# A new order of the steps in a kernel of sliding-window attention and a two-layer MLP

## The chip, the cores and the metric

The kernel runs on one core of one Trainium2 chip. A core has a matrix engine (TensorE, PE in the profile), three engines for elementwise work (VectorE = DVE, ScalarE = ACT, GpSimd = POOL) and SyncE (SP), which here only issues DMAs. Each engine takes its own instructions strictly in order; semaphores let one engine wait for another or for a transfer. TensorE writes its results into PSUM, eight banks of 512 f32 columns on 128 partitions; everything else on the core lies in SBUF. The metric is the device time of one execution in microseconds (us).

## The reference

```python
B, H, S, D = 8, 8, 576, 64          # q, k, v: f32
scores = (1 / sqrt(D)) * q @ k.T     # per batch and head
mask = (rel >= 0) & (rel < 64)       # rel = query position - key position
attn = softmax(where(mask, scores, -1e9))
x = (attn @ v).transpose(0, 2, 1, 3).reshape(B * S, H * D)     # 4608 x 512
h = x @ w_in                         # w_in 512 x 2048
g = h - tanh(h)
out = g @ w_out                      # w_out 2048 x 512, out f32
```

A query sees itself and the 63 keys before it. The token rows that attention gives are the input of the MLP.

## The kernel before

**Tiling.** Heads go in pairs: batch b has four pairs, g = 4b to 4b + 3, 32 in all. A pair's 576 queries are nine windows of 64, and a window needs the 128 keys up to its end. The 4608 tokens of the MLP are nine chunks c of 512, and the 2048 hidden columns are 16 tiles m of 128. All products are in bf16, with f32 in PSUM. Batch b fills tokens 576b to 576b + 575, so chunk c needs the batches up to the one that holds its last token: chunk 4, for example, spans batches 3 and 4.

**Stages of a batch.** Loads go through GpSimd's DMA queue and turn f32 into bf16 on the way for batches 3 to 7. Batches 0 to 2 turn keys and queries round with TensorE (steps Fp, Ep) and copy them out of PSUM (Fc, Ec); the rows that lk, lq load for a pair are rearranged by ck, cq first (function cast, L126; called casts below). Batches 3 to 7 load token rows (lr for keys, qr for queries, L166, the second number being one of five blocks of 128 tokens) and turn them round by DMA transposes on SyncE's queue (tk, L171, into kw; tq, L179, into qw). LV (L145) loads a block of values, and Z, za, zb (L151, L152, function move) copy the rows that windows need on the other half of the partitions. tz copies the tail of q.

**Steps on TensorE.** S.g (L299, L304) makes the scores of pairs g and g + 1 of batches 3 to 7; Rp (L286) those of one pair and half of its windows in batches 0 to 2. PP.g (L348) multiplies the probabilities of two pairs by the values. Xp (L397) turns attention rows round for batches 0 to 2; from batch 3 on Y.b.half (L416, two DMA transposes each) does so on SyncE's queue. H.c.m (L431) is the first layer of chunk c and tile m: four matmuls of 512 columns, with PSUM bank m mod 2 for c > 1. Hp.c.m.half (L508) is one half of such a step, which needs only one half of the chunk's columns (Y.b.0 or Y.b.1). W.c.s.part (L474) is a quarter of the second layer for 128 tokens: four matmuls of 512 columns into bank 2; the quarters of one s can come in any order. The last s of the last chunk is cut by columns (L467).

**Steps on the other engines.** ScalarE: A.c.m (tanh, L439), Sx.g.part (the exp of parts 0, 1 and, of the ninth window, 2; L314), Rx (L318). VectorE: G.c.m (h - tanh(h), L445, which frees H's bank), M.g (masking the probabilities in place, L323), DR.g and DN.g.n (reciprocal, three normalisations, L365, L368). O.c.s.engine copies a finished second-layer tile out of PSUM on ScalarE (L90) or VectorE (L92), and SyncE stores it (L495; three buffers). Xc, Fc, Ec, ck, cq, za, zb and tz name their engine as their last letter: a ScalarE, v VectorE, p GpSimd.

**What sets the order.** Nothing is scheduled by a program: one long string, PLAN (from L537, played by play, L532), lists the steps. Each word is a step, looked up in STEPS (L518), and its instructions go to the end of their engine's queue, DMAs to that of SyncE or GpSimd. The string thus fixes the order on every engine; the waits between engines follow from the buffers that the steps share.

```python
    def play(script):
        for word in script.split():
            what, *args = word.split(".")
            STEPS[what](*[ENG[a] if a in ENG else int(a) for a in args])
```

The lines that matter below: the end of chunk 0's first layer (L554), the casts ck.9 to cq.11 (L557 to L562), tz.3 (L571), batch 5's transposes tk.5, tq.5 with Y.4 (L579 to L585), and Sx.22, which begins behind A.4.4 (L590).

Of the kernel before, what the change touches and what calls it, by code (L numbers as in the profile page):

```python
# [15 lines left out]
def kernel(  # L16
# [515 lines left out]
    def play(script):  # L532
# [30 lines left out]
        A.1.3 Rx.10.1.3 H.1.4 A.1.4 G.1.3 Ec.11.6.a H.1.5 A.1.5 qr.3.0 Z.2 H.1.6 qr.3.2 PP.8 G.1.5 Rp.11.0.3
        A.1.6 tk.3.1 tq.3.3 lr.3.0 H.1.8 Rx.11.0.3 G.1.4 G.1.6 DR.8 H.1.7 DN.8.2 A.1.8 A.1.7 H.1.9 tq.3.1 G.1.8
        H.1.11 G.1.7 A.1.9 tk.3.4 H.1.10 lr.3.3 A.1.11 A.1.10 DN.8.1 G.1.9 Rp.11.1.3 Rx.11.1.3 Rp.10.0.6 tq.3.2
        G.1.11 DN.8.0 G.1.10 Rx.10.0.6 H.1.12 tq.3.0 M.10 H.1.14 A.1.12 M.11 H.1.13 Xp.2.0.1.3 Xp.2.0.0.4 G.1.12
        A.1.13 A.1.14 Xc.2.0.1.3.a PP.10 H.1.15 LV.4.1 LV.3.1 A.1.15 Xc.2.0.0.4.a LV.3.3 G.1.13 LV.3.2 LV.3.0
# [5 lines left out]
        M.13 tk.4.3 tq.4.4 G.2.5 A.2.4 PP.12 W.1.2.3 H.2.7 lr.6.4 lr.5.4 DR.12 DN.12.2 G.2.4 tq.4.3 tk.4.2
        tq.4.1 lr.6.3 DN.12.0 A.2.7 lr.5.3 lr.5.1 lr.5.0 tq.4.2 DN.12.1 H.2.6 G.2.7 qr.5.2 S.14 H.2.9 A.2.6
        Sx.14.2 Sx.14.1 A.2.9 tk.5.4 Sx.14.0 G.2.6 G.2.9 M.14 M.15 qr.6.0 W.1.2.0 H.2.8 W.1.2.1 W.1.2.2
        Xp.3.0.1.3 A.2.8 G.2.8 tq.5.3 H.2.11 O.1.2.v PP.14 DR.14 H.2.10 A.2.11 A.2.10 Xc.3.0.1.3.v G.2.10
        Xp.3.0.0.4 W.1.3.2 G.2.11 tq.5.4 W.1.3.3 H.2.12 A.2.12 H.2.13 Z.4 A.2.13 W.1.3.1 G.2.12 G.2.13 H.2.14
# [73 lines left out]
```

## Time and profile before

| | |
|---|---|
| median of 3 runs | 307.63 us (307.45 to 307.67) |
| the profiled execution: span from the first to the last instruction | 305.2 us |
| TensorE busy | 297.8 us, 98% |
| VectorE busy | 176.2 us, 58% |
| ScalarE busy | 157.5 us, 52% |
| GpSimd busy | 103.7 us, 34% |
| granted TensorE clock | 1.000 |
| moved by DMA | 36.77 MB, mean 120 GB/s |

The profile is of one execution; all durations below are from it, and its span is the time from its first to its last instruction. PE is TensorE's matmuls, PEld its weight loads, which run beside the matmul in front. An entry such as "L474 PE MATMUL ps<-w_out_sb,gT" names the line of the kernel, the engine, the operation, and output <- inputs by the program's names. In a list of groups, "xN | busy, mean ns | idle before, releaser" gives a group's count, its busy time, the mean of one, and the idle time of the engine in front of it with what ended most of it. In a timeline the first number is the start in us from the span's start, the second what the row's instructions took together, and [..] an idle time before them. A matmul's end is modelled, so matmul records overlap. SPq and POOLq are the DMA queues' issuing instructions.

### The profile page before, as it was taken

To read this page: it belongs to the slowest core of one execution; us is meant where nothing else is said; L and a number is where in the kernel's file an instruction comes from. 1 tells how busy PE (TensorE), PEld (TensorE's weight loads), DVE (VectorE), ACT (ScalarE), POOL (GpSimd) and SP (SyncE) were. 2 spreads that over 40 slices of the span, in tenths; PEclk is the share of its full clock that TensorE was granted. 3 is DMA by queue.
4 is the path that set the end of the run, shared out by engine and by line. 5 is a ranking of instruction groups with operands and counts; after the bars stand their busy time and mean duration, and the time that the engine had idled before them with its cause. 6 is when DMAs were issued, how large, how long until landed. Compare 5 with 4: busy or idle time off the path is not lost.

```text
span 305.2 us, 6469 instructions
## 1 busy us (share of the span) xinstructions
PE 297.8 (98%) x2599; PEld 149.4 (49%) x2632; DVE 176.2 (58%) x316; ACT 157.5 (52%) x265; POOL 103.7 (34%) x141
## 2 busy tenths in 40 slices
...
DMA packets 132878, 36.77 MB, mean 120 GB/s; under 512 B 119920, under 2 KB 127344, under 8 KB 132848
## 3 DMA queue, kind: packets, MB, share of 16 engines
q0 software_dynamic: 92752, 18.06, 85.3%
...
HBM read 36.70 MB, written 9.44 MB: 151 GB/s over the span
## 4 chain that ended last, share of the span: by engine, by line
PE 87%; DVE 5%; ACT 3%; issue 2%; POOL 2%; DVEq 0%; ACTq 0%; POOLq 0%
PE ps L474 38%; PE ps L431 30%; PE ps L508 6%; PE ps L348 3%; PE ps L304 2%; DVE gT L445 2%; PE ps L397 1%; ACT th L439 1%; PE ps L286 1%; PE ps L467 1%; DVE pt L323 1%; PE ps L260 1%; PE ps L281 1%; PE ps L227 1%; POOL qall L110 1%
## 5 line engine op out<-in xcount | busy, mean ns | idle before, releaser
L445 DVE TENSOR_TENSOR gT<-ps,th 128x512 bf16<-128x512 f32 x144 | 97.2, 687 | 85.3 <-ACT th L439 84.6
L474 PE MATMUL ps<-w_out_sb,gT 128*128 128x512 bf16 x527 | 131.5, 380 | 2.2 <-issue 0.8
L439 ACT ACTIVATE th<-ps 128x512 f32<-128x512 f32 x144 | 84.7, 599 | 93.0 <-PE ps L431 79.7
L431 PE MATMUL ps<-xT,wi 128*128 128x512 bf16 x496 | 120.7, 380 | 0.1
L474 PEld LDWEIGHTS <-gT 128*128 128x128 bf16 x560 | 53.3, 98 | 61.4
L431 PEld LDWEIGHTS <-wi 128*128 128x128 bf16 x496 | 47.0, 98 | 54.3
L145 POOL DMA_DIRECT2D vw<-in_v_dram x35 | 30.0, 872 | 36.1 <-PE ps L348 33.5
L90 ACT ACTIVATE ysb<-ps 128x512 f32<-128x512 f32 (+1 forms) x24 | 14.2, 593 | 30.9 <-PE ps L474 30.2
L166 POOL DMA_DIRECT2D qall<-in_q_dram x25 | 21.7, 881 | 24.1 <-DMA qw<-qall 21.4
L166 POOL DMA_DIRECT2D kall<-in_k_dram x25 | 21.7, 875 | 10.4 <-DMA kw<-kall 4.8
L314 ACT ACTIVATE pt<-ps 128x1024 bf16<-128x1024 f32 (+1 forms) x30 | 23.3, 816 | 3.5 <-PE ps L304 3.2
L323 DVE TENSOR_TENSOR pt<-pt,ps 128x1152 bf16<-128x1152 bf16 x28 | 20.5, 749 | 5.1 <-ACT pt L314 3.2
L508 PE MATMUL ps<-xT,wi 128*128 128x512 bf16 x80 | 20.8, 380 | 0.0
L92 DVE COPY ysb<-ps 128x512 f32<-128x512 f32 (+1 forms) x11 | 7.1, 650 | 20.5 <-PE ps L467 13.2
L368 DVE TENSOR_TENSOR xs<-ps,rcp 128x384 bf16<-128x384 f32 x28 | 15.2, 550 | 0.3
L318 ACT ACTIVATE pt<-ps 128x640 bf16<-128x640 f32 (+1 forms) x24 | 14.7, 659 | 0.8 <-PE ps L286 0.8
L348 PEld LDWEIGHTS <-pt 128*64 128x64 bf16 x504 | 9.4, 112 | 6.3 <-DVE pt L323 2.1
L90 ACT ACTIVATE kt<-ps 128x576 bf16<-128x576 bf16 x10 | 6.5, 647 | 10.8 <-PE ps L256 6.8
L227 PE MATMUL ps<-warm 128*128 128x512 bf16 (+1 forms) x35 | 10.6, 435 | 1.1 <-DVE warm L207 1.1
L508 PEld LDWEIGHTS <-wi 128*128 128x128 bf16 x80 | 7.4, 98 | 8.5 <-issue 0.4
L348 PE MATMUL ps<-vw,pt 128*64 128x65 bf16 x504 | 11.0, 197 | 0.3 <-DVE pt L323 0.2
L365 DVE TENSOR_TENSOR xs<-ps,rcp 128x384 bf16<-128x384 f32 x14 | 7.7, 550 | 0.1
...
## 6 DMA issues: line engine op xcount, KB each, us to landing
...
vw<-in_v_dram POOLq DMA_DIRECT2D x28, 128.0 KB, 6.6
qall<-in_q_dram POOLq DMA_DIRECT2D x20, 128.0 KB, 7.5
kall<-in_k_dram POOLq DMA_DIRECT2D x20, 128.0 KB, 6.8
...
```

The source lines that it names most:

```text
L90: nc.scalar.activation(o, i, ACT.Copy)
L145: nc.gpsimd.dma_start(out=w[:, 2 * i + 1, :, 0:D] if i < NF else w[64:128, 2 * i, :, 0:D], in_=v[b, :, 128 * i:128 * i + n].rearrange("h p ...
L166: nc.gpsimd.dma_start(out=token_rows(b, n)[0:c, i], in_=(q if n == "q" else k)[b, :, 128 * i:128 * i + c].rearrange("h p d -> p h d"))
L314: nc.scalar.activation(o, sp, ACT.Exp, scale=scale)
L323: nc.vector.tensor_tensor(p, p, mask.unsqueeze(1).to_broadcast([128, 2 * NJ, 64]), ALU.mult)
L348: nc.tensor.matmul(ps[r, bank, 65 * i:65 * i + 65], PT[(g + r2) % NPT][:, j, r], vw[b % 2][:, j, p0 + r2 + NP * h, :], start=True, stop=True)
L368: nc.vector.tensor_tensor(xs[b % 2][:, p0 // 2, 0:6, n // 2, :], ov[:, :, 0:D], sums[g][:, n].to_broadcast([128, 6, D]), ALU.mult)
L431: nc.tensor.matmul(hp, w_in_tile(ki, m), chunk_tile(c)[:, n.start // 64:n.stop // 64, ki % 2, 64 * (ki // 2):64 * (ki // 2) + 64], start=( ...
L439: nc.scalar.activation(th[:, n], hp, ACT.Tanh)
L445: nc.vector.tensor_tensor(gT[c][:, m, columns(s)], hp, th, ALU.subtract)
L474: nc.tensor.matmul(yp, gT[c][:, m, s * 128:(s + 1) * 128], w_out_sb[:, m, :], start=n == 1 and i == 0, stop=n == 4 and i == 3)
L508: nc.tensor.matmul(hp, w_in_tile(half + 2 * i, m), chunk_tile(c)[:, :, half, 64 * i:64 * i + 64], start=n == 1 and i == 0, stop=n == 2 and ...
```

## The change

The first 230 words of PLAN stay. From "H.0.14 M.4" on (end of chunk 0's first layer, 37.6 us into the profiled span) all words come in a new order. They are the same steps with the same matmuls, transfers and buffers, but for three things: some steps go to another engine, some to another PSUM bank, and score steps of batch 2 are paired differently. Other engines: the casts ck.9, ck.10, ck.11 go from ScalarE to GpSimd and cq.10, cq.11 from VectorE to GpSimd; zb.1.3 from GpSimd to ScalarE, zb.1.2 from ScalarE to VectorE; tz.5 from VectorE and tz.6 from ScalarE to GpSimd, tz.7 from VectorE to ScalarE; and many of the copies O, Xc, Fc and Ec change between ScalarE and VectorE. The loads and transposes of batches 3 to 7 stand in longer runs of DMA steps between the others, and the quarters of the second layer stand in other places between first-layer steps.

```diff
-        Rx.7.1.3 cq.9.v H.0.14 M.4 wo.3 zb.1.3.p G.0.12 Ec.8.1.a PP.4 wo.1 A.0.14 H.0.15 mk DR.4 DN.4.1 G.0.14
-        A.0.15 H.0.13 DN.4.0 za.1.3.a W.0.0.0 Rp.8.0.3 G.0.15 A.0.13 Rp.8.1.5 DN.4.2 zb.1.2.a za.1.2.v Rx.8.1.5
-        W.0.1.0 M.7 qr.3.3 LV.2.3 lk.11.p PP.6 Rx.8.0.3 Xp.1.0.1.3 W.0.0.2 G.0.13 Xp.1.0.0.4 DR.6 Xc.1.0.1.3.a
-        DN.6.2 DN.6.0 W.0.1.2 DN.6.1 Xp.1.1.0.5 lk.10.p ck.9.a Xc.1.0.0.4.a Fp.9.3 Xc.1.1.0.5.a Xp.1.1.1.4
-        lr.3.2 lq.10.p lq.11.p LV.2.2 Hp.1.0.0 Ep.9.7 Xc.1.1.1.4.v Ec.9.7.a Fc.9.3.a Hp.1.0.1 W.0.1.3 W.0.0.3
-        qr.3.4 LV.2.0 Rp.9.1.5 Rp.9.0.3 LV.2.1 W.0.0.1 O.0.0.a M.8 LV.2.4 W.0.1.1 lr.3.1 lr.3.4 A.1.0 tq.3.4
-        G.1.0 O.0.1.a Rx.9.1.5 Rx.9.0.3 ck.11.a M.9 ck.10.a W.0.2.1 W.0.2.0 W.0.2.3 W.0.2.2 W.0.3.2 qr.3.1
...
-        Hp.1.2.1 Hp.1.2.0 Fc.10.7.a A.1.1 A.1.2 Rp.10.1.3 G.1.1 cq.11.v G.1.2 Fc.11.5.a H.1.3 Ep.11.6 tk.3.2
...
-        W.1.1.2 G.2.3 Hp.2.1.0 tz.3.a Hp.2.1.1 W.1.1.3 G.2.0 qr.4.2 qr.5.4 lr.5.2 H.2.2 A.2.1 G.2.1 S.12 A.2.2
...
-        G.2.14 W.2.0.2 Xc.3.1.1.7.v Xc.3.0.0.4.a Xc.3.1.0.6.a G.2.15 qr.5.0 Hp.3.0.0 W.2.0.3 Hp.3.1.1 Hp.3.1.0
-        O.2.0.a A.3.1 W.2.1.1 Hp.3.0.1 W.2.1.2 G.3.1 tz.4.v A.3.0 S.16 Sx.16.2 W.2.1.3 Sx.16.1 G.3.0 H.3.3
-        W.2.1.0 M.17 Sx.16.0 M.16 H.3.2 A.3.3 PP.16 G.3.3 O.2.1.a A.3.2 tk.5.2 qr.5.1 qr.6.4 H.3.5 LV.5.3
-        W.2.2.1 DR.16 A.3.5 tk.5.1 DN.16.2 tq.5.2 G.3.2 DN.16.1 H.3.4 DN.16.0 Y.4.0 A.3.4 S.18 G.3.5 W.2.2.0
-        H.3.7 G.3.4 Sx.18.1 A.3.7 Sx.18.2 G.3.7 W.2.2.3 H.3.6 A.3.6 Sx.18.0 tk.6.4 tk.5.3 tq.5.0 tq.5.1 H.3.9
-        tk.5.0 M.19 W.2.2.2 G.3.6 qr.7.1 H.3.8 M.18 A.3.9 PP.18 A.3.8 O.2.2.v G.3.9 DR.18 G.3.8 DN.18.2 DN.18.1
-        DN.18.0 W.2.3.0 W.2.3.3 H.3.11 qr.6.2 lr.6.0 LV.5.4 lr.6.2 LV.5.0 A.3.11 W.2.3.1 G.3.11 Y.4.1 tq.6.4
-        H.3.10 W.2.3.2 A.3.10 tq.6.2 G.3.10 O.2.3.a H.3.13 H.3.14 A.3.13 LV.5.1 LV.5.2 lr.6.1 qr.6.1 A.3.14
-        G.3.13 W.3.0.2 H.3.15 tz.5.v G.3.14 qr.6.3 H.3.12 W.3.0.0 A.3.15 G.3.15 Hp.4.1.0 A.3.12 G.3.12 Hp.4.1.1
-        A.4.1 W.3.0.1 G.4.1 W.3.0.3 Hp.4.0.1 H.4.3 Hp.4.0.0 O.3.0.v tk.6.3 tk.6.2 A.4.0 S.20 A.4.3 Sx.20.2
-        Sx.20.0 Sx.20.1 tq.6.0 tk.6.0 W.3.1.1 G.4.0 G.4.3 W.3.1.0 H.4.2 W.3.1.3 A.4.2 S.22 G.4.2 H.4.4 W.3.1.2
-        H.4.7 A.4.4 G.4.4 M.20 O.3.1.a Sx.22.0 Sx.22.1 A.4.7 W.3.2.1 H.4.6 W.3.2.2 A.4.6 Sx.22.2 W.3.2.3 Z.5
-        G.4.7 M.22 M.21 H.4.9 PP.20 G.4.6 tq.7.1 tq.6.1 A.4.9 tk.6.1 tq.6.3 W.3.2.0 O.3.2.a DR.20 DN.20.2 G.4.9
...
-        W.8.1.0 W.8.2.3 W.8.2.0 W.8.2.1 O.8.1.a W.8.3.2 O.8.2.a O.9.0.a W.8.3.0 W.8.3.1 O.8.3.v"""
+        Rx.7.1.3 cq.9.v H.0.14 M.4 Ec.8.1.a PP.4 wo.3 G.0.12 Rp.8.0.3 A.0.14 Rx.8.0.3 H.0.15 A.0.15 wo.1 lk.11.p
+        lq.10.p LV.2.2 qr.4.3 LV.2.4 qr.3.0 ck.9.p ck.11.p LV.2.1 LV.2.0 lk.10.p cq.10.p lq.11.p qr.4.4 LV.2.3
+        lr.3.4 lr.3.0 qr.3.4 ck.10.p cq.11.p lr.3.1 DR.4 G.0.14 DN.4.1 DN.4.2 DN.4.0 G.0.15 Ep.9.4 za.1.3.a
+        zb.1.3.a H.0.13 A.0.13 Ec.9.4.a za.1.2.v zb.1.2.v M.7 W.0.0.0 Xp.1.0.0.6 Xp.1.0.1.3 W.0.1.0 Xc.1.0.0.6.a
...
+        A.1.13 qr.3.1 LV.3.2 lr.4.0 qr.3.2 tq.4.3 LV.3.4 LV.3.0 qr.4.2 qr.3.3 lr.3.2 tq.3.1 tq.3.2 lr.3.3 LV.3.3
+        lr.4.4 LV.3.1 lr.4.1 tk.3.4 tq.3.4 LV.4.3 qr.4.1 qr.5.4 tk.3.1 tq.3.3 tq.3.0 tk.3.2 tk.3.3 tk.3.0 LV.4.2
+        qr.5.2 qr.4.0 lr.4.2 lr.5.0 tq.4.1 tq.4.4 lr.5.1 qr.5.3 LV.4.0 qr.5.1 lr.4.3 tk.4.0 tk.4.4 G.1.8 G.1.12
+        H.1.14 H.1.15 Xc.2.0.1.4.a G.1.13 Xp.2.0.0.3 W.1.0.1 W.1.0.2 A.1.14 A.1.15 tz.3.a Xc.2.0.0.3.a DR.10
+        G.1.14 DN.10.0 DN.10.2 Xp.2.1.0.7 Xc.2.1.0.7.a G.1.15 W.1.0.0 Hp.2.1.0 DN.10.1 Xp.2.1.1.7 Xc.2.1.1.7.a
...
+        M.17 G.3.7 M.16 Z.4 G.3.2 W.2.2.0 W.2.2.2 W.2.2.1 H.3.3 A.3.3 PP.16 H.3.8 DR.16 DN.16.0 G.3.3 W.2.2.3
+        A.3.8 H.3.9 G.3.8 DN.16.1 DN.16.2 O.2.2.a A.3.9 lr.5.4 lr.5.3 qr.6.2 LV.5.1 qr.6.0 lr.6.2 LV.5.4 LV.5.3
+        LV.5.2 qr.5.0 qr.6.3 lr.5.2 lr.6.1 qr.6.1 LV.5.0 lr.6.0 G.3.9 H.3.6 A.3.6 G.3.6 S.18 Sx.18.2 W.2.3.2
+        H.3.5 Sx.18.0 A.3.5 W.2.3.3 H.3.10 G.3.5 Sx.18.1 A.3.10 W.2.3.1 tq.5.2 tk.5.3 tk.5.2 tq.5.1 tq.5.0 Y.4.0
+        tk.5.4 lr.6.4 lr.6.3 M.18 Z.5 M.19 H.3.11 A.3.11 W.2.3.0 PP.18 G.3.11 DR.18 DN.18.1 G.3.10 DN.18.0
+        DN.18.2 Y.4.1 tk.6.4 tq.6.1 tk.6.1 LV.6.2 lr.7.2 qr.7.3 tq.6.0 tk.6.3 tk.6.2 tq.6.3 H.3.13 O.2.3.a
+        A.3.13 G.3.13 W.3.0.1 H.3.14 W.3.0.2 H.3.15 A.3.14 G.3.14 A.3.15 H.3.12 A.3.12 G.3.15 G.3.12 S.20
+        Sx.20.2 Sx.20.0 Sx.20.1 Hp.4.1.0 W.3.0.0 W.3.0.3 Hp.4.1.1 Hp.4.0.1 Hp.4.0.0 S.22 A.4.1 A.4.0 G.4.1 G.4.0
+        O.3.0.v H.4.9 A.4.9 H.4.2 A.4.2 G.4.2 G.4.9 M.21 M.20 W.3.1.3 W.3.1.0 W.3.1.2 H.4.3 H.4.4 W.3.1.1
+        Sx.22.2 Sx.22.1 A.4.3 A.4.4 G.4.3 G.4.4 H.4.7 H.4.6 A.4.7 A.4.6 O.3.1.v G.4.6 PP.20 DR.20 DN.20.2 G.4.7
+        W.3.2.0 H.4.10 A.4.10 DN.20.1 G.4.10 Sx.22.0 M.22 DN.20.0 M.23 W.3.2.2 H.4.5 A.4.5 G.4.5 W.3.2.1 H.4.8
+        W.3.2.3 A.4.8 lr.7.3 LV.6.1 qr.7.1 lr.7.1 qr.7.0 qr.7.4 qr.6.4 tq.7.4 tq.6.4 tq.7.3 LV.6.4 lr.7.0 PP.22
+        G.4.8 tk.6.0 lr.7.4 tk.7.4 tk.7.2 tq.6.2 LV.6.3 tk.7.3 O.3.2.v H.4.14 A.4.14 G.4.14 DR.22 H.4.11 A.4.11
...
+        W.8.1.1 W.8.1.0 W.8.2.0 W.8.2.3 W.8.1.3 O.8.2.a W.8.0.0 W.8.0.1 W.8.0.3 W.8.1.2 O.8.1.a W.8.3.2 W.8.0.2
+        W.8.3.3 O.8.0.v O.9.0.a W.8.3.1 W.8.3.0 O.8.3.a"""
```

More of the change, by code (lines that the diff above doesn't have):

```diff
@@ L563 @@
[L563 to L567, printed above, removed]
@@ L573 @@
[L573 to L577, printed above, removed]
```

77 lines of the change are left out of this document (43 added, 34 removed).

## The prediction

> **What bounds the kernel now.** I read the page first (span, busy shares, chain), then the timeline of the weight loads, because a matmul's record hides waits: records overlap, while a weight load starts once per matmul.
>
> ```profile
> span 305.2 us, 6469 instructions
> ...
> PE 297.8 (98%) x2599; PEld 149.4 (49%) x2632; DVE 176.2 (58%) x316; ACT 157.5 (52%) x265; POOL 103.7 (34%) x141
> ...
> PE 87%; DVE 5%; ACT 3%; issue 2%; POOL 2%; DVEq 0%; ACTq 0%; POOLq 0%
> ```
>
> TensorE sets the end. The next question is how much of its 298 us is waiting in disguise.
>
> ```profile
> 161.99 0.10 PEld L431 LDWEIGHTS <-wi 128*128 128x128 bf16 x1
> 162.51 0.66 PEld L348 LDWEIGHTS <-pt 128*64 128x64 bf16 x36 [0.42 <-issue]
> 163.20 0.55 PEld L474 LDWEIGHTS <-gT 128*128 128x128 bf16 x4
> 163.87 1.18 PEld L431 LDWEIGHTS <-wi 128*128 128x128 bf16 x6
> ...
> 285.06 5.06 PEld L474 LDWEIGHTS <-gT 128*128 128x128 bf16 x24
> 290.24 1.29 PEld L467 LDWEIGHTS <-gT 128*128 128x128 bf16 x8
> ```
>
> From 285.06 to 290.24 are 24 matmuls: 0.216 us each, so a step of four (H or W) is 0.863 us. A PV step (PP) starts 0.52 us after the last wide load instead of 0.216 (0.30 for the change of form), lasts 0.69, and the step behind it takes 0.67 instead of 0.863: net 0.80. Against these prices the waits stand out:
>
> ```profile
> 43.41 0.93 PEld L348 LDWEIGHTS <-pt 128*64 128x64 bf16 x36 [0.42 <-issue]
> ...
> 66.11 0.65 PEld L348 LDWEIGHTS <-pt 128*64 128x64 bf16 x36 [0.55 <-DVE vw L152]
> ...
> 90.14 0.36 PEld L348 LDWEIGHTS <-pt 128*64 128x64 bf16 x18 [0.47 <-DVE pt L323]
> 90.80 0.36 PEld L348 LDWEIGHTS <-pt 128*64 128x64 bf16 x18 [0.30 <-DVE pt L323]
> ```
>
> PP.6 takes 0.93 for 0.66 (0.27 lost), PP.8 begins 0.13 late, PP.12 loses 0.05 and 0.30. That is 0.75 us; I allow up to 1.1 for smaller gaps that I do not list. So from chunk 0's last steps on, the old order leaves TensorE waiting for about 0.8 us. **This is all that a new order can win**, since the same matmuls are issued.
>
> **The change part by part.** *TensorE's own work.* Counting runs of attention matmuls in both orders: 28 before, 27 after, because the score steps of batch 2 are paired differently and some stand right behind a PP. One change of form fewer is 0.3 at most; one old run stands behind transposes, a cheaper start, so I take -0.1 (bounds 0 and -0.3). The end (last quarter's columns, one small copy, one store) has the same steps in other clothes: 0.
>
> *The old waits.* I assume that all of them go: -0.8 (bounds 0 and -1.1).
>
> *A new wait at H.4.7.* In the new order ScalarE has "Sx.22.2 Sx.22.1 A.4.3 A.4.4" behind A.4.2. By the waits of the built kernel Sx.22.2 waits for M.20, in both orders; before, it stood behind A.4.7 and A.4.6, where this cost nothing. Now two tanhs are queued behind it, for them G.4.3, and for G.4.3 the bank of H.4.7.
>
> ```profile
> 147.05 1.29 DVE L445 TENSOR_TENSOR gT<-ps,th 128x512 bf16<-128x512 f32 x2 [1.66 <-ACT th L439]
> 156.90 1.42 DVE L323 TENSOR_TENSOR pt<-pt,ps 128x1152 bf16<-128x1152 bf16 x2
> ...
> 153.68 1.94 ACT L314 ACTIVATE pt<-ps 128x1024 bf16<-128x1024 f32 x2
> 155.49 1.11 ACT L439 ACTIVATE th<-ps 128x512 f32<-128x512 f32 x2
> 156.44 0.43 ACT L314 ACTIVATE pt<-ps 128x256 bf16<-128x256 f32 x1
> ...
> 280.10 1.89 PE L474 MATMUL ps<-w_out_sb,gT 128*128 128x512 bf16 x7
> 280.30 0.60 ACT L439 ACTIVATE th<-ps 128x512 f32<-128x512 f32 x1 [0.27 <-PE ps L431]
> 280.93 0.69 DVE L445 TENSOR_TENSOR gT<-ps,th 128x512 bf16<-128x512 f32 x1 [0.17 <-ACT th L439]
> ```
>
> The last three rows give the hand-over: a tanh starts 0.20 after the next step's matmuls have begun, lasts 0.60, the subtract follows after 0.03 and lasts 0.69. Back to back, subtracts and masks advance by 0.60 to 0.67 (two in 1.29, two in 1.42), a wide exp by 0.91. From the end of H.4.2 as zero: A.4.2 0.20 to 0.80; G.4.2 from 0.83, G.4.9 from 1.43, M.21 from 2.03, M.20 from 2.70 to 3.45; Sx.22.2 from 3.48, Sx.22.1 from 3.80, A.4.3 from 4.74 to 5.34; G.4.3 to 6.06. TensorE meanwhile has W.3.1.3, W.3.1.0, W.3.1.2, H.4.3, H.4.4 and W.3.1.1: 6 x 0.863 = 5.18. H.4.7 is late by **0.9**. (Were Sx.22.2 free earlier, this would be nothing.)
>
> *Batch 5's hand-over (S.20 and Hp.4.1.1).* SyncE's queue is in order. In the new order the transposes tq.5.2, tk.5.3, tk.5.2, tq.5.1, tq.5.0, two of Y.4.0 and tk.5.4 all stand behind the store O.2.2, that is behind W.2.2.3.
>
> ```profile
> 191.31 5.12 SPq L171 DMA_TRANSPOSE kw<-kall  x4
> 196.53 1.22 SPq L179 DMA_TRANSPOSE qw<-qall  x1
> ...
> 160.65 0.34 SPq L495 DMA_DIRECT2D out_dram<-ysb  x1
> 161.08 2.54 SPq L416 DMA_TRANSPOSE xT<-xs  x2
> ...
> 150.47 0.22 PE L299 MATMUL ps<-q,kw 128*128 128x64 bf16 x2
> 150.62 0.70 PE L304 MATMUL ps<-qw,kw 64*128 64x64 bf16 x34
> 151.25 1.04 PE L431 MATMUL ps<-xT,wi 128*128 128x512 bf16 x4
> ```
>
> A transpose takes 5.22 / 4 = 1.30 of the queue, a store 0.43, an S step 0.78. From the end of W.2.2.3: the copy O.2.2 ends at 0.80, its store is issued at 0.83, tk.5.4 at 1.26 + 7 x 1.30 = 10.4. S.20 wants it after 15 steps of 0.863, S.18 and PP.18: 14.5. It may take 4.1 to land. Y.4.1 follows PP.18's last norm (PP.18 ends at 9.55, and DR, three norms and G.3.10 take 2.4): issued at 12.0, wanted by Hp.4.1.1 at 14.5 + 0.78 + 0.43 + 2 x 0.863 = 17.5, so 5.5 to land. What do they take? Loads on GpSimd's queue decide:
>
> ```profile
> qw<-qall SPq DMA_TRANSPOSE x1, 2.4
> kw<-kall SPq DMA_TRANSPOSE x1, 2.4
> ...
> xT<-xs SPq DMA_TRANSPOSE x1, 4.9
> ...
> xT<-xs SPq DMA_TRANSPOSE x2, 6.0
> ...
> qw<-qall SPq DMA_TRANSPOSE x1, 6.6
> ...
> 135.91 1.76 POOL L166 DMA_DIRECT2D qall<-in_q_dram  x2 [21.40 <-DMA qw<-qall]
> ...
> 163.41 4.18 POOL L145 DMA_DIRECT2D vw<-in_v_dram  x5 [18.06 <-PE ps L348]
> ```
>
> These are windows of the DMA view: 133:135.4 (the first two), 136:137.3, 137.35:138.7, 138.8:140. A burst of loads starts at 135.91: in front of it transposes land in 2.4, just behind its start in 4.9, then in 6.0 to 6.6. In the new order the first load of a burst (LV.6.2) waits for PP.18, at 9.55: the start of a burst again follows a PV step, as at 163.41. So tk.5.4, 0.4 into the burst, takes about 4.9 (0.8 late) and Y.4.1, two into it, 6.0 to 6.6 (0.5 to 1.1 late, in place of the 0.8 and not on top). I take **0.9**; bounds 0 (all land in 2.4) and 2.5.
>
> *The same one batch later.* Y.5.0 and Y.5.1 are issued into the burst behind PP.22; by the same count they are 0 to 1.2 late for Hp.5.0.0; I take **0.4**.
>
> *Batch 2 and 3 loads.* Five casts go from ScalarE and VectorE to GpSimd, and ck.11, ck.10 and cq.11 there wait for loads to land, with all later loads queued behind them. At the far end ScalarE waits in tz.3.a for transpose tq.3.4, and Xc.2.0.0.3.a, which Hp.2.1.0 needs, is queued behind it.
>
> ```profile
> L92 POOL COPY vw<-vw 64x520 bf16<-64x520 bf16 x4 | 2.5, 620 | 2.3 <-DMA vw<-in_v_dram 2.2
> ...
> kall<-in_k_dram POOLq DMA_DIRECT2D x2, 128.0 KB, 8.7
> qall<-in_q_dram POOLq DMA_DIRECT2D x1, 128.0 KB, 8.1
> ```
>
> No cast on GpSimd is in this trace; from the copy, 0.62 for 520 elements, 768 elements are an estimated 0.9 each (bounds: 0.6, the copy itself, and twice 0.9). Loads beside transposes took 8.1 to 8.7 (window 58:60), else some 6 in the page's medians. With 0.9 and 7 I find the chain just in time at Hp.2.1.0; with 9 it is over 2 late. I take **0.3** (bounds 0 and 3). ScalarE and VectorE get room where the casts leave, but they are no bound there.
>
> [...]
>
> *Short bank waits in chunk 1* (H.1.12, where VectorE has subtracts, norms and a mask in a row): 0 to 0.4, taken 0.2.
>
> **Sum:** -0.8 - 0.1 + 0.9 + 0.9 + 0.4 + 0.3 + 0.2 = +1.8 us. The profiled span goes from 305.2 to 307.0; the median of the runs, 307.63, lies 2.4 above that span, and I keep this distance: **309.4 us**.
>
> **The rivals.**
> 1. *The transposes land in time*: bursts start a little later or the queue drains faster, as in the rows of 2.4. Then the old waits are only exchanged for H.4.7 and chunk 1: -0.9 + 0.9 + 0.2 = +0.2, 307.8 us. For it: 4.9 against 4.1 allowed is a near thing. Against: the burst is tied to PP.18.
> 2. *The other side, faster*: M.20 comes early enough that Sx.22.2 does not hold the tanhs, and transposes land in time too. The point is 0.9 us on M.20. Then only -0.9 remains, with a little left of chunk 1: 306.8 us at -0.8. Against: VectorE's five instructions from A.4.2 on have no gap to give.
> 3. *GpSimd's chain fails*: casts of 1.8 us, or blocked by VectorE, put 5 x 0.9 = 4.5 us on the load queue; some 2 of it are covered before Ep.11.7 and Hp.2.1.0. It decides from about 1 us. That is +2.5 on the forecast: 311.9 us. For it: three waits for landings in a row. Against: the four copies of 0.62 agree with each other although VectorE was busy beside them.
>
> [...]
>
> **How the numbers follow.** Forecast 0.45 (308.4 to 310.5), rival 1 0.27, rival 2 0.10, rival 3 0.18. A difference of 0.2% (0.6 us) is about what a measurement of this kernel can tell. Rival 2 is faster by more than that (0.10); rival 1 lies within it except for a tenth of it (0.24); the rest is slower (0.66). The range 307.0 to 311.9 leaves out rival 2 and the upper half of rival 3.
>
> **What would show it.** In the profile after: a gap in front of H.4.7's matmuls near 154 us with ScalarE's small exp waiting for L323; S.20 and Hp.4.1.1 waiting for DMA kw and xT near 141 to 146; ScalarE idle near 77 in front of the q copy. PP.6, PP.8 and PP.12 at 0.66 to 0.7 would show the old waits gone. I am wrong if transposes near a burst's start land in 2.4, if GpSimd's casts differ much from 0.9, or if a wait shows up at S.12 or S.16, where I count none.

## The result, and the profile after

The changed kernel takes 321.33 us (median of 4 runs, 320.19 to 322.74) against 307.65 us: 1.043 times the time before, 95% interval 1.040 to 1.047. That is 13.7 us slower, where 1.8 were forecast and 311.9 was the upper end of the range. The profiled execution took 322.74 us, the longest of the four, and its span is 15.7 us longer than that of before. Here and below, a kernel's time is the median of its fast runs, which leaves out single executions more than 1.5% above its fastest, and each ratio is taken against runs of the kernel before from the same session.

The page of the changed kernel, the rows that answer to those of before:

```profile
span 320.9 us, 6508 instructions
...
PE 306.4 (95%) x2632; PEld 151.5 (47%) x2632; DVE 177.5 (55%) x311; ACT 155.3 (48%) x264; POOL 109.3 (34%) x147
...
PEclk9999999999799999997899979999999999999999
...
PE 62%; DMA 21%; POOL 6%; SPq 4%; issue 3%; DVE 1%; ACT 1%; POOLq 0%; ACTq 0%
```

Two things are new. Transfers hold 21% of the chain that sets the end, where before it was 87% TensorE and no DMA. (This share alone proves little: p4_loads below, as fast as the kernel before, has 14%.) And the granted clock dips in three places. The same row of the kernel before:

```profile
PEclk9999999999999999999999999999999999999999
```

What TensorE waited for in the changed kernel (total, times, longest), then its weight loads around the four long waits:

```profile
PE ps L508 <- DMA xT<-xs: 3.4, 1, 3.4
PE ps L299 <- DMA kw<-kall: 3.0, 1, 3.0
PE ps L508 <- ACT xT L90: 2.0, 1, 2.0
```

```profile
81.97 0.10 PEld L508 LDWEIGHTS <-wi 128*128 128x128 bf16 x1 [2.33 <-issue]
...
84.09 0.15 PEld L508 LDWEIGHTS <-wi 128*128 128x128 bf16 x1 [0.28 <-issue]
...
148.92 0.13 PEld L299 LDWEIGHTS <-kw 128*128 128x128 bf16 x2 [3.49 <-DMA kw<-kall]
...
151.04 0.15 PEld L474 LDWEIGHTS <-gT 128*128 128x128 bf16 x1 [0.28 <-issue]
...
164.47 1.39 PEld L431 LDWEIGHTS <-wi 128*128 128x128 bf16 x7 [0.98 <-issue]
...
187.69 0.10 PEld L508 LDWEIGHTS <-wi 128*128 128x128 bf16 x1 [3.67 <-issue]
```

The numbers in brackets are the gaps in front of weight loads (PEld), which TensorE starts ahead of the matmuls (before S.20 the last weight load ended at 145.42, the last matmul at 145.92). In order they are those of Hp.2.1.0, S.20, H.4.7 and Hp.5.0.0. Of each gap 0.1 is there in any case (a load takes 0.10, and the next starts 0.216 after it), so they cost 2.2, 3.4, 0.9 and 3.6: 10.1 us. The rows at 84.09 and 151.04 show the rest: a weight load behind the wait starts 0.43 after the one before it (0.28 of gap and 0.15) instead of 0.216. TensorE works at half speed there. The windows view says from when to when; its last columns are the granted clock, the DMA share and GB/s:

```profile
83.00:83.50 0.50, 0.50 (x3) 0.20 (x2) 0.00 (x0) 0.50 (x2) 0.50 (x1) 0.59 1.71 158
86.25:86.50 0.25, 0.25 (x2) 0.13 (x1) 0.25 (x1) 0.00 (x0) 0.00 (x0) 0.50 2.27 148
86.50:86.75 0.25, 0.25 (x2) 0.10 (x1) 0.07 (x1) 0.00 (x0) 0.00 (x0) 0.99 1.84 206
147.50:148.00 0.50, 0.00 (x0) 0.00 (x0) 0.00 (x0) 0.00 (x0) 0.50 (x2) 0.95 2.21 165
154.40:154.80 0.40, 0.40 (x2) 0.15 (x1) 0.00 (x0) 0.00 (x0) 0.00 (x0) 0.53 3.63 131
188.50:189.00 0.50, 0.50 (x3) 0.20 (x2) 0.00 (x0) 0.00 (x0) 0.00 (x0) 0.91 2.17 165
192.25:192.50 0.25, 0.25 (x2) 0.10 (x1) 0.00 (x0) 0.25 (x1) 0.00 (x0) 0.86 0.88 176
```

A slice's mean gives the moment: 0.59 over 83.0 to 83.5 means that the clock fell from 1.00 to 0.50 at 83.09. It is at half from 83.09 to 86.50, 147.95 to 154.78 and 188.91 to 192.32: 3.41, 6.83 and 3.41 us, four stretches of one length. Less the 0.97 that TensorE still stood at S.20, it worked 12.7 us at half clock, which can cost 6.3 at most; 15.7 less the 10.1 of the waits leaves 5.6. The cost of the half clock can also be read directly, by timing the same steps of TensorE in an execution in which the clock stayed at 1.00: behind Hp.2.1.0 they took 4.55 us (2.86 in e1_tz3), from S.20 to S.22 6.55 (3.88 in p4_loads), behind Hp.5.0.0 4.93 (3.39 in p4_loads). That is 1.7, 2.7 and 1.5 us more, 5.9 in all. Waits and half clock thus make 16.0, beside the 15.7 measured. The small ones nearly cancel: of the old waits PP.12's is gone and PP.6's is not, and in chunk 1 the two Rp.10 steps cost 0.64 and the two of Rp.11 0.71, where two such steps cost 0.47 in the kernel before: 0.2 new each.

### The profile page after: what moved, and what is told of

Same layout as the page of the kernel before. It is cut to its first block, busy times and chain, and to the rows that moved or that the text cites. A ratio compares the mean times of both kernels' runs of the same rounds, so it can differ in the third digit from the quotient of the medians.

```text
span 320.9 us, 6508 instructions
## 1 busy us (share of the span) xinstructions
PE 306.4 (95%) x2632; PEld 151.5 (47%) x2632; DVE 177.5 (55%) x311; ACT 155.3 (48%) x264; POOL 109.3 (34%) x147
## 4 chain that ended last, share of the span: by engine, by line
PE 62%; DMA 21%; POOL 6%; SPq 4%; issue 3%; DVE 1%; ACT 1%; POOLq 0%; ACTq 0%
PE ps L474 29%; PE ps L431 22%; DMA wi<-in_moe_w_in_dram 5%; PE ps L508 4%; DMA qall<-in_q_dram 4%; DMA kall<-in_k_dram 3%; DMA xT<-xs 3%; DMA qw<-qall 2%; DMA vw<-in_v_dram 2%; PE ps L304 2%; SPq L179 2%; POOL vw L145 2%; DMA kw<-kall 2%; PE ps L348 2%; SPq L171 2%
## 5 line engine op out<-in xcount | busy, mean ns | idle before, releaser
L474 PE MATMUL ps<-w_out_sb,gT 128*128 128x512 bf16 x560 | 139.0, 386 | 0.0
L431 PE MATMUL ps<-xT,wi 128*128 128x512 bf16 x496 | 121.2, 379 | 1.0 <-DVE gT L445 0.9
L474 PEld LDWEIGHTS <-gT 128*128 128x128 bf16 x560 | 54.4, 99 | 64.4 <-issue 3.6
L145 POOL DMA_DIRECT2D vw<-in_v_dram x35 | 30.8, 889 | 16.1 <-PE ps L348 14.6
L508 PE MATMUL ps<-xT,wi 128*128 128x512 bf16 x80 | 23.0, 406 | 5.4 <-DMA xT<-xs 3.4
L92 DVE COPY ysb<-ps 128x512 f32<-128x512 f32 x17 | 11.7, 688 | 27.8 <-PE ps L474 27.8
L90 ACT ACTIVATE ysb<-ps 128x512 f32<-128x512 f32 (+2 forms) x18 | 10.3, 573 | 28.0 <-PE ps L474 24.6
L368 DVE TENSOR_TENSOR xs<-ps,rcp 128x384 bf16<-128x384 f32 x28 | 14.9, 550 | 0.2
L92 POOL COPY q<-qw 64x256 bf16<-64x256 bf16 x2 | 0.8, 398 | 33.7 <-DMA qw<-qall 33.7
L90 ACT ACTIVATE xT<-ps 128x512 bf16<-128x512 bf16 (+3 forms) x17 | 7.3, 486 | 4.4 <-PE ps L397 3.4
```

Of the source, the lines that this page charges most:

```text
L90: nc.scalar.activation(o, i, ACT.Copy)
L145: nc.gpsimd.dma_start(out=w[:, 2 * i + 1, :, 0:D] if i < NF else w[64:128, 2 * i, :, 0:D], in_=v[b, :, 128 * i:128 * i + n].rearrange("h p ...
L431: nc.tensor.matmul(hp, w_in_tile(ki, m), chunk_tile(c)[:, n.start // 64:n.stop // 64, ki % 2, 64 * (ki // 2):64 * (ki // 2) + 64], start=( ...
L474: nc.tensor.matmul(yp, gT[c][:, m, s * 128:(s + 1) * 128], w_out_sb[:, m, :], start=n == 1 and i == 0, stop=n == 4 and i == 3)
L508: nc.tensor.matmul(hp, w_in_tile(half + 2 * i, m), chunk_tile(c)[:, :, half, 64 * i:64 * i + 64], start=n == 1 and i == 0, stop=n == 2 and ...
```

## The experiments

My theory: the transfers stand where they land too late, and each long wait costs a half-clock stretch on top. Rivals: each late transfer is a separate accident; the clock falls for another reason; the new compute order itself asks for the impossible; the casts on GpSimd are to blame.

### One wait undone at a time

**e1_tz3.**

```diff
-... tz.3.a Xc.2.0.0.3.a ... Xc.2.1.1.7.a mk
+... Xc.2.0.0.3.a ... Xc.2.1.1.7.a tz.3.a mk
```

> The changed kernel with one word moved: tz.3.a (ScalarE, the copy that waits for transpose tq.3.4) goes from in front of Xc.2.0.0.3.a to behind Xc.2.1.1.7.a. In the changed kernel Hp.2.1.0 stood 2.2 us behind it, and from 83.1 to 86.5 us TensorE's granted clock was 0.50. Theory (each wait also costs the half-clock stretch that follows it, about 1.7 us): both go, 321.3 - 3.9 = 317.4 us, and the windows view shows a clock of 1.00 from 80 to 90. Rival A (the low clock comes for a reason of its own): only the wait goes, 319.1. Rival B (batch 3's transposes are late for every reader): S.12 waits instead, 321.

Measured: 318.87 us, ratio 1.039 (1.032 to 1.046), which overlaps the changed kernel's 1.040 to 1.047. Hp.2.1.0 no longer waits, and the clock is 1.00 from 60 to 90 us, as the theory said; but rival B comes true in part. The waits of e1_tz3:

```profile
PE ps L299 <- DMA kw<-kall: 3.5, 1, 3.5
PE ps L508 <- DMA xT<-xs: 2.1, 2, 1.7
PE ps L304 <- DMA kw<-kall: 1.6, 1, 1.6
```

The 1.6 at L304 is new: S.12, which had been spared because TensorE came to it later, now waits for tk.3.0. The 3.5 at L299 is S.20, and it speaks against the theory as I put it: TensorE's matmuls and the window around them show no half clock behind it.

```profile
142.38 1.89 PE L431 MATMUL ps<-xT,wi 128*128 128x512 bf16 x8
147.79 0.23 PE L299 MATMUL ps<-q,kw 128*128 128x64 bf16 x2 [3.52 <-DMA kw<-kall]
```

```profile
148.00:155.00 7.00, 6.89 (x96) 3.78 (x98) 1.98 (x3) 4.25 (x7) 2.75 (x4) 1.00 1.88 125
```

So not each long wait costs a half-clock stretch. The last section sets this one beside those that did.

**e2_tk54.**

```diff
-... W.2.3.1 tq.5.2 tk.5.3 tk.5.2 tq.5.1 tq.5.0 Y.4.0 tk.5.4 ...
+... W.2.3.1 tk.5.4 tq.5.2 tk.5.3 tk.5.2 tq.5.1 tq.5.0 Y.4.0 ...
```

> The changed kernel with tk.5.4 moved in front of tq.5.2, so that SyncE issues it first of its run of transposes, about 10 us earlier. Theory (two waits one behind the other): S.20 no longer waits 3.5 us, but the first half of Y.4.1, which landed at 151.2 in the changed kernel, is then late by about 2.8 for Hp.4.1.1, and a half-clock stretch follows it too: 321.3 - 1.5 = 319.8 us. Rival (tk.5.4 is the only late transfer here): 3.5 us of wait and some 2.5 of low clock go, 315.3.

Measured: 319.61 us, ratio 1.040 (1.031 to 1.049). The theory's 319.8 is met, but the interval holds that of the changed kernel: a gain is not shown. S.20 is cured, and the two halves of chunk 4's first step wait in its place, for Y.4.0 and Y.4.1. Weight loads of e2_tk54:

```profile
147.78 0.11 PEld L508 LDWEIGHTS <-wi 128*128 128x128 bf16 x2 [1.80 <-DMA xT<-xs]
...
153.02 0.96 PEld L508 LDWEIGHTS <-wi 128*128 128x128 bf16 x5 [3.18 <-issue]
```

So behind a late transfer stands another that is late too. Whether they share a cause is what the next run asks.

**e3_gate.**

```diff
+    def after_x(c, i):
+        nc.gpsimd.tensor_copy(seen_x, chunk_tile(c)[0:64, i:i + 2, 1, :])
...
-... tk.6.1 LV.6.2 lr.7.2 ...
+... tk.6.1 gx.5.3 LV.6.2 lr.7.2 ...
```

> The changed kernel with one small copy added on GpSimd ahead of LV.6.2 (64 x 256 bf16, it reads what the second transfer of Y.4.1 wrote), so that the burst of 14 loads that starts at 140.8 us starts only when Y.4.1 has landed. The transposes are issued as before. Theory (loads beside them make transposes land late): tk.5.4 and Y.4.1 land 2.4 to 3 us after their issue instead of 5.8 to 7.7, S.20 and Hp.4.1.1 wait at most 0.3, no half clock near 150: 321.3 - 6 = 315.3 us. Rival (transposes issued back to back hold each other up, whatever the loads do): landing times stay at 5 to 7 us, 321.

Measured: 325.83 us, ratio 1.056 (1.049 to 1.063), slower, and yet the theory's landing times hold. The DMA view of the changed kernel for 143 to 144.3 us and 144.3 to 145.6, then of e3_gate for 144 to 145.4 and 145.4 to 146.7:

```profile
kw<-kall SPq DMA_TRANSPOSE x1, 5.8
...
xT<-xs SPq DMA_TRANSPOSE x1, 6.8
```

```profile
kw<-kall SPq DMA_TRANSPOSE x1, 2.3
...
xT<-xs SPq DMA_TRANSPOSE x1, 2.4
```

The same two transposes, tk.5.4 and the first of Y.4.1, issued one behind the other as before; without the loads beside them they land in 2.3 and 2.4 us instead of 5.8 and 6.8. Neither S.20 nor Hp.4.1.1 waits. The time went elsewhere: the loads held back are late for batch 6.

```profile
PE ps L308 <- DMA qw<-qall: 10.3, 1, 10.3
PE ps L512 <- ACT xT L91: 3.2, 1, 3.2
```

S.24 waits 10.3 us for tq.6.2, which was issued into the next burst (the second row is Hp.2.1.0, as in the changed kernel). A gate without room behind it only moves the loss.

### What a wait costs beside its length

**e4_fill.**

```diff
-... Hp.2.1.0 ... S.20 ... Hp.5.0.0 ...
+... U.10.4 Hp.2.1.0 ... U.15.3 S.20 ... U.15.3 Hp.5.0.0 ...
```

> The changed kernel with matmuls added whose result nobody reads: 10 in front of Hp.2.1.0 (into bank 4), 15 in front of S.20 and 15 in front of Hp.5.0.0 (into bank 3), of 512 columns each, so 2.2, 3.2 and 3.2 us of work at the places where TensorE waited 2.3, 3.5 and 3.7 us. The waits themselves stay. Theory (the clock is halved because TensorE stood idle): the granted clock stays at 1.00 and the time falls by what the half clock cost, 321.3 - 5 = 316.3 us. Rival (the clock is halved for another reason, such as load on the chip or the DMA traffic): no gain, or a loss of up to 0.5 where the added work outlasts the wait, 321.3 to 321.8.

Measured: 319.78 us, ratio 1.036 (1.029 to 1.043), clock 0.995 to 1.00 in its runs against 0.979 to 0.989 in the changed kernel's. The clock moves as the theory says; the gain is 1.6 and not 5, and not clear of the noise (the changed kernel's interval is 1.040 to 1.047). In the profiled run S.20 waited 2.0 us beyond the 3.2 of added work, and one half-clock stretch, from 150.9 on, followed. So the price was measured where no load or transpose runs, in chunks 7 and 8 of the kernel before:

```diff
+    def hold(c, m, n):
+        for i in range(n):
+            nc.gpsimd.tensor_copy(later, gT[c][:, m, 0:128]) if i < n - 1 else nc.gpsimd.tensor_copy(late, gT[c][:, m, 0:128])
+    def held():
+        nc.tensor.matmul(ps[:, 5, 0:128], late, warm, start=True, stop=True)
...
-... G.7.9 H.7.8 W.6.1.0 ...
+... G.7.9 wt.7.9.N H.7.8 W.6.1.0 wl ...
```

The word wt plays hold, N small copies on GpSimd behind a subtract; wl plays held, a matmul that needs the last of them. N is 4 in i1_idle1 and 7 in the other two, and i3_filled has U.11.4, eleven matmuls that nobody reads, ahead of wl.

> The kernel before with four waits added on TensorE in chunks 7 and 8, where no load or transpose runs: a chain of 4 small copies on GpSimd (128 x 128) that starts when one subtract is done, and a small matmul that needs the last of them. Each should let TensorE stand for about 1.2 us. Theory (a short wait costs its own length only): 4 x 1.2 = 5 us more than the kernel before, granted clock 1.00. Rival (every wait lowers the clock): 5 + 4 x 1.7 = 12 us more.

> As i1_idle1 with 7 copies in each chain, so four waits of about 2.4 us. Theory (a wait of over 2 us is followed by a stretch of 3.4 us at half clock, which costs 1.7 us): 4 x (2.4 + 1.7) = 16 us more than the kernel before if each is long enough, at least two of the four in any run. Rival (the clock does not depend on the wait): 9.6 us more, clock 1.00.

> As i2_idle2 with 11 matmuls of 512 columns ahead of each waiting one, into a bank that nobody reads, so that TensorE works for 2.4 us where it stood. Theory (idleness lowers the clock): 9.6 us more than the kernel before and a granted clock of 1.00, so 3 to 7 us less than i2_idle2. Rival (the clock does not depend on the wait): the same as i2_idle2.

Measured, against 308.07 before: i1_idle1 313.27 (ratio 1.017, 1.014 to 1.019), i2_idle2 320.28 (1.039, 1.036 to 1.043), i3_filled 317.12 (1.030, 1.028 to 1.033). The four waits of i2_idle2 (weight loads), and the windows at the begin and the end of the half clock behind the third and behind the fourth:

```profile
248.54 0.10 PEld L484 LDWEIGHTS <-late 128*128 128x128 bf16 x1 [2.54 <-POOL late L481]
...
257.81 0.10 PEld L484 LDWEIGHTS <-late 128*128 128x128 bf16 x1 [2.62 <-POOL late L481]
...
273.97 0.10 PEld L484 LDWEIGHTS <-late 128*128 128x128 bf16 x1 [2.62 <-POOL late L481]
...
286.65 0.10 PEld L484 LDWEIGHTS <-late 128*128 128x128 bf16 x1 [2.62 <-POOL late L481]
```

```profile
274.00:274.50 0.50, 0.50 (x3) 0.30 (x4) 0.00 (x0) 0.00 (x0) 0.00 (x0) 0.70 0.96 365
277.50:278.00 0.50, 0.50 (x3) 0.20 (x2) 0.00 (x0) 0.46 (x1) 0.00 (x0) 0.88 0.00 0
287.50:288.00 0.50, 0.50 (x4) 0.20 (x2) 0.00 (x0) 0.22 (x1) 0.00 (x0) 0.86 0.00 0
291.00:291.50 0.50, 0.50 (x3) 0.23 (x2) 0.00 (x0) 0.00 (x0) 0.00 (x0) 0.73 0.00 0
```

Short waits cost their length (5.2 for four gaps of 1.5 in the weight loads, of which 0.1 is there anyway), with a clock of 0.998 or more. Of the four longer ones, two were followed by half clock and two of the same length were not; the four cost 12.2 us idle and 9.1 filled. Where two of four waits are followed by a stretch, 3.2 us make about 1.6 for one; the six runs of i2_idle2 had clocks of 0.988 to 0.993, which stands for one to two stretches, so this is an estimate. It agrees with the 1.7 and 1.5 read directly above. That idleness brings the half clock on is shown (i3_filled, with work in place of it, had clocks of 0.999 and 1.000 in its four runs); that each long wait does is not, and the last section compares the four waits.

### Compute order and transfers exchanged; the casts

**f1_dmaB, f2_dmaA, f3_dmaB_sx22** each put one kernel's transfers at their places among the other's compute steps; f3 moves Sx.22.2 as well.

> The order of the changed kernel on TensorE, and of all other compute steps, with the transfers put back: every lr, qr, LV, lk, lq, tk, tq, Y and wo, the casts ck, cq and the copies tz (these with their engines of before) stand where they stood in the kernel before, by the same amount of TensorE work done ahead of them, except where a buffer they need is not free there yet. Theory (the loss comes from where the transfers stand; a wait undone alone uncovers the next late transfer): no wait for a DMA is longer than 0.5 us and none lowers the clock, H.4.7 keeps its 0.9, chunk 1's small waits keep their 0.4 or so: 307.6 + 1.3 = 308.9 us. Rival (the new compute order itself wants things earlier than any placing of the transfers can give): waits of 2 us and more for DMA stay, 315 or more.

> The reverse: the kernel before with its compute order, and the same set of words (transfers, casts, tz) placed as in the changed kernel. Theory (the loss comes from where the transfers stand): TensorE waits for transposes at batches 3, 5 and 5's output, with half clock after the longer waits, +8 to +14 us: 316 to 322. Rival (the compute order makes the loss): 308 to 310.

> As f1_dmaB, and Sx.22.2 moved from in front of Sx.22.1 to behind A.4.4. Theory (Sx.22.2 waits for M.20 and holds A.4.3 and A.4.4): H.4.7 starts without a wait, 0.9 us less than f1_dmaB. Rival (M.20 itself is late for Sx.22.1 as well, or H.4.7's bank waits for another reason): the same as f1_dmaB.

Measured: 334.8 (ratio 1.089, 1.085 to 1.093), 344.95 (1.121, 1.115 to 1.127) and 334.66 us (1.086, 1.082 to 1.090). Both exchanges are worse than either kernel: the theory as I put it falls. The largest wait of f1_dmaB and VectorE in front of it:

```profile
PE ps L348 <- DVE pt L323: 10.3, 1, 10.3
```

```profile
148.81 0.70 DVE L151 COPY vw<-vw 64x2080 bf16<-64x2080 bf16 x1 [10.71 <-DMA vw<-in_v_dram]
```

Z.5, which stands ahead of M.19 in the new order, waits 10.7 us for batch 5's values, which the old places load later; M.19 and PP.18 stand behind it. So f1 is no clean test of the compute order: Z.5 is a copy on VectorE and kept its new place, while the loads that it needs went back. In f2 (its profiled execution took 348.1 us) TensorE waits 11.7 us in three waits for output transposes, 9.0 for a query transpose and 5.5 for a subtract of VectorE. A mixture of the two orders thus says little about either; the runs of p below take that up. In f3, H.4.7 no longer waits (0.86 in f1), which the times hide.

**f4_casts.**

```diff
-ck.9.a ck.10.a ck.11.a cq.10.v cq.11.v
+ck.9.p ck.10.p ck.11.p cq.10.p cq.11.p
```

> The kernel before with one part of the change alone: ck.9, ck.10, ck.11, cq.10 and cq.11 on GpSimd, at their places in the string. Theory (a cast takes GpSimd 0.82 us, as in the changed kernel, and delays the loads behind it by that and by its wait for a landing, which the old places of the transfers can bear): within 0.6 us of the kernel before. Rival (the third rival of the prediction: casts blocked by VectorE, or the loads behind them too late): 2 us slower or more.

Measured: 307.94 us, ratio 1.001 (0.999 to 1.003). A cast on GpSimd in the changed kernel, three and two of them:

```profile
L92 POOL COPY kb<-kall 96x768 bf16<-96x768 bf16 x3 | 2.5, 843 | 3.8 <-DMA kall<-in_k_dram 3.8
...
L92 POOL COPY qb<-qall 96x768 bf16<-96x768 bf16 x2 | 1.7, 833 | 0.7 <-DMA qall<-in_q_dram 0.7
```

0.84 each. The casts alone, among the old order's steps and transfers, cost nothing that can be measured.

### The transfers put right, the compute order kept

**p1_batch3, p2_nosx, p2_all, p4_loads, p5_early**, each on top of the one before (p4 on p2_all, p2_nosx without the move of Sx.22.2):

```diff
+p1: ... tq.3.0 tk.3.0 tk.3.4 tq.3.4 tk.3.1 tq.4.3 ... tq.3.1 tq.3.2 ...
+p2: ... lr.6.3 qr.6.4 ... Y.4.1 ... gx.5.3 LV.6.2 ... tq.6.4 tk.6.0 tq.6.2 O.2.3.a
+p2: ... LV.6.3 LV.6.0 qr.7.2 ... DN.20.0 Y.5.0 ... Y.5.1 gx.6.4 LV.7.1 ... tq.7.4 ...
+p2_all: Sx.22.1 A.4.3 A.4.4 Sx.22.2
+p4: ... qr.3.1 qr.3.2 qr.3.3 lr.3.2 lr.3.3 LV.3.2 ... O.2.3.a tq.6.4 tk.6.0 tq.6.2
+p5: lk.11.p lq.10.p lk.10.p lq.11.p LV.2.2 ... lr.4.0 qr.4.3 qr.4.4 ... tk.3.3 tq.4.3
```

> The changed kernel with five transposes of batch 3 moved: tq.3.0, tk.3.0, tk.3.4, tq.3.4 and tk.3.1, whose loads have landed by 64.5 us, go in front of tq.4.3, tq.3.1 and tq.3.2, which wait for loads that land at 66.9 to 70.7; nothing else. e1_tz3 had only moved the wait: Hp.2.1.0 was cured, and S.12 then waited 1.7 us for tk.3.0. Theory (SyncE's queue stands behind the late loads, and that makes all of batch 3 late): tq.3.4 lands near 71 instead of 81 and tk.3.0 near 70 instead of 90, neither Hp.2.1.0 nor S.12 waits, the clock stays at 1.00 up to 145: 321.3 - 3.9 = 317.4 us. Rival (the late part is something that this does not move): S.12 or Hp.2.1.0 waits over 1 us, 319 or more.

> p1_batch3, with batch 5, 6 and 7 put right in the same manner: the copy on GpSimd of e3_gate ahead of LV.6.2, a second one ahead of LV.7.1 that waits for Y.5.1, so that neither burst of loads runs beside the transposes that TensorE waits for; qr.6.4 loaded ahead of the first burst, LV.6.0 and qr.7.2 at its end; tq.6.4, tk.6.0 and tq.6.2 issued ahead of the store O.2.3, Y.5.0 behind DN.20.0, and the five tq.7, tk.7 that stood ahead of Y.5.0 behind Y.5.1. The compute steps keep the order of the changed kernel. Theory (the new compute order is as good as the old one once the transfers stand right): the waits of over 1 us are gone and with them the half clock; what is left against the kernel before is 0.9 at H.4.7 and some 0.4 in chunks 0 and 1: 307.7 + 1.3 = 309.0 us. Rival (the compute order itself wants transfers earlier than they can be): waits of 2 us and more stay, 313 or more.

> As p2_nosx, with Sx.22.2 moved from in front of Sx.22.1 to behind A.4.4. Theory (Sx.22.2 waits for M.20 and holds the tanhs behind it): H.4.7 does not wait, 0.9 us less than p2_nosx, 308.1. Rival (H.4.7's bank is late anyway): the same as p2_nosx.

> p2_all with two places changed where it still waited: S.12 (2.6 us for tk.3.3, whose load lr.3.3 took 12 us behind five loads that nobody wants yet), so qr.3.2, qr.3.3, lr.3.2 and lr.3.3 go directly behind qr.3.1 on GpSimd's queue; and W.3.3.3 (1.6 us: O.3.2's buffer waits for the store O.2.3, which p2 had put behind three transposes), so these three go behind O.2.3. Theory (the loss is the place of the transfers alone): no wait over 0.5 us is left, 312.3 - 4.2 = 308.1 us, within 0.3% of the kernel before. Rival (each cure uncovers another late transfer): 310 or more.

> p4_loads with batch 2's loads put first on GpSimd's queue (lk.10, lq.11 ahead of LV.2.2; qr.4.3 and qr.4.4, which batch 4 wants 25 us later, and transpose tq.4.3 behind batch 3's). p4_loads still waits some 2 us in chunks 0 to 2: PP.6 0.4, Rp.10 0.9, PP.8 0.6, S.16 0.4. Theory (these waits too are loads that stand behind ones nobody wants yet): Rp.10 and PP.8 no longer wait, 308.5 - 1.2 = 307.3 us, 0.3% under the kernel before. Rival (they come from the order of the steps on ScalarE and VectorE): the same as p4_loads.

| | us | ratio (95%) | what still waits |
|---|---|---|---|
| p1_batch3 | 317.50 | 1.031 (1.025 to 1.038) | S.12 1.4, S.20, Hp.5.0.0 |
| p2_nosx | 310.71 | 1.009 (1.006 to 1.012) | S.12 2.1, PP.6 1.1, H.4.7 0.9, W.3.3.3 0.9 |
| p2_all | 312.33 | 1.013 (1.009 to 1.016) | S.12 2.7, W.3.3.3 1.6; H.4.7 no more |
| p4_loads | 308.52 | 1.002 (1.000 to 1.004) | H.1.4 0.6, S.16 and PP.6 0.4 |
| p5_early | 312.11 | 1.012 (1.009 to 1.015) | S.16 2.5 and a half-clock stretch behind it; PP.6 and H.1.4 0.4 |

The page and the waits of p4_loads, to set beside those of the changed kernel:

```profile
span 306.4 us, 6479 instructions
...
PEclk9999999999999999999999999999999999999999
```

```profile
PE ps L478 <- issue: 0.8, 5, 0.2
PE ps L435 <- DVE gT L449: 0.7, 2, 0.5
...
PE ps L303 <- DMA kw<-kall: 0.2, 1, 0.2
```

With the transfers put right and the compute order kept but for Sx.22.2, the time cannot be told from that of before, and the clock row has no dip. The small waits listed are those of the profiled executions. On the way p1 and p2 each uncovered a wait for a transfer (S.12 for tk.3.3) or made one (W.3.3.3, whose buffer waits for a store that I had put back).

Three forecasts on the way need a second look. p1's 317.4 came out (317.50), though S.12 still waits 1.4 us, so the number was in part luck. In p2_all the wait at H.4.7 went, as the theory said, but the time did not fall to 308.1: 312.33 against 310.71, with intervals that overlap. The waits at S.12 and W.3.3.3 were longer there, and three of its six runs had a clock of 0.994 or 0.995. And the 0.9 that the expectation of p5 gives to Rp.10 is no wait: from the last wide weight load in front of it to the first behind it is 0.89 in the kernel before, the changed kernel and p4_loads alike. The 0.6 that it gives to PP.8 stands at H.1.4.

p5_early missed its 307.3: batch 4's transposes came too late for S.16. PP.6 and H.1.4 still wait although batch 2's loads now stand first, which speaks for the rival (the order on ScalarE and VectorE); it was not tried further.

**b1_pp**, the kernel before with PP.12 and PP.6 one step later:

```diff
-... PP.12 W.1.2.3 ... PP.6 Rx.8.0.3 Xp.1.0.1.3 ...
+... W.1.2.3 PP.12 ... Rx.8.0.3 Xp.1.0.1.3 PP.6 ...
```

> The kernel before with two steps moved back by one on TensorE: PP.12 behind W.1.2.3 and PP.6 behind Xp.1.0.1.3, where the kernel before waited 0.42 and 0.29 us for masks and copies. Theory (those waits are all that an order can win here): both go, -0.7 at most, 307.0 us, within 0.3% of the kernel before. Rival (what stands behind them, DR.12 and DR.6 on VectorE, is then as late): no change.

Measured: 308.90 us, ratio 1.003 (1.001 to 1.005), slightly slower. PP.12's wait is gone, and H.2.6 waits 0.6 for a subtract of VectorE in its place; Xp.1.0.1.3, now in front, waits 1.0 for an exp that frees its bank. No version beat both kernels.

## Why the prediction was wrong

The direction was right, the size was not: 1.8 us forecast, 13.7 measured. The step that failed is the landing time of transposes issued beside a burst of loads. Both terms that rest on it were far too small: S.20 and Hp.4.1.1 (0.9 taken, 3.4 measured) and Hp.5.0.0 (0.4 taken, 3.6 measured), because landings of 4.9 to 6.6 us were taken and 5.8 to 9.2 came. A second term was put at nothing without a reason: that TensorE's clock falls to half behind such waits, 5.6 to 5.9 us.

- *H.4.7*: forecast 0.9, measured 0.86, and gone when Sx.22.2 moves (p2_all, f3). This step was right in place, mechanism and size.
- *S.20 and Hp.4.1.1*: forecast 0.9, bounds 0 and 2.5; measured 3.4 and two half-clock stretches. TensorE came to S.20 at 145.4, 0.3 from where I had put it. The queue was later (tk.5.4 issued 11.9 after the end of W.2.2.3 and not 10.4, since tk.5.3 held the queue 2.3 instead of 1.3), and it took 5.8 to land and not 4.9. The upper bound of 2.5 was taken from the slowest row of before, 6.6; in the changed kernel transposes took up to 9.2.
- *Hp.5.0.0*: forecast 0.4, measured 3.6, and one half-clock stretch. I took 6.0 to 6.6 for landings behind a burst's start; Y.5.0 took 9.2. This term failed most.
- *Batch 3's loads*: forecast 0.3, bounds 0 and 3; measured 2.2, at the place and by the chain that I named (tz.3.a waits for tq.3.4, Xc.2.0.0.3.a stands behind it). The loads landed as I had taken them (medians of 6.7 to 7.1 between 60 and 73 us, 7 taken). The transpose tq.3.4 was late: three others ahead of it (tq.4.3, tq.3.1, tq.3.2) held SyncE's queue from 61.96 to 71.92 waiting for their loads, so that it was issued at 73.3, and it took 7.6 to land (80.9). p1_batch3, which puts it ahead of those three, takes the wait away. The half clock behind it, 1.7, came on top.
- *Casts*: estimated 0.9, measured 0.84, no loss by themselves (f4). The third rival falls: no run shows a cast of 1.8 us or one that VectorE blocks; the three and two of the changed kernel took 0.84 and 0.83 on average.
- *The old waits*: forecast -0.8; PP.12's 0.35 went, PP.6 still takes 0.90, and Rp.10 and Rp.11 lose 0.4 in chunk 1, where I had put 0.2.
- *What was not in the sum at all*: the half clock, 5.6 to 5.9 us. Every wait was priced at its own length.

None of the signs that I had named for being wrong showed in the changed kernel: no transpose near a burst's start landed in 2.4, the casts took about 0.9, and S.12 and S.16 did not wait. No sign was named for the clock.

p4_loads comes near to the first rival's world, transposes that land in time: 308.52 against the 307.8 that the rival gave. But the agreement does not confirm the small terms. p4_loads moves Sx.22.2 and so has no 0.9 at H.4.7; without it the sum gives about -0.7, and p4_loads is 0.45 above the 308.07 of its own session. The small terms were about 1.1 too favourable, chiefly because the old waits did not all go (PP.6 0.4, and new ones of 0.6 at H.1.4 and 0.4 at S.16).

The length of a gap alone does not tell whether the clock falls. In the weight loads, gaps of 2.33 us (Hp.2.1.0) and 2.62 (the last two of i2_idle2) were followed by half clock, and gaps of 2.54 and 2.62 (its first two) were not; nor was S.20's of 3.5 us between matmuls in e1_tz3.
